# Five small moves in a recurrent attention kernel: halves of a cast, an order of matmuls, filler units, load order, a last projection

## The chip, the cores and the metric

The kernel runs on one core of a Trainium2 chip. The metric is the device time of one execution in microseconds; it is compared by the median of several runs on the same chip. In what follows PE is the matmul engine (TensorE), PEld its weight loads, ACT is ScalarE, DVE is VectorE, POOL is GpSimd, and SP is the engine that issues most of the DMAs.

## The reference

Two branches over the same x of 2048 tokens by 512 are mixed by a gate per token. Branch A is attention with a memory of 8 rows, which is carried from one segment of 32 tokens to the next; branch B is a channel MLP.

```python
g = _sigmoid((x * gate_w).sum(-1, keepdims=True))
# A: 64 segments, one after the other
h = jnp.concatenate([mem, xs], axis=1)            # 8 + 32 rows of 512
q, k, v = (jnp.einsum('btd,dhe->bhte', h, W) for W in (Wq, Wk, Wv))   # 32 heads of 128
scores = jnp.where(mask, jnp.einsum('bhqe,bhke->bhqk', q, k) * scale, -1e9)
o = jnp.einsum('bhqk,bhke->bhqe', _softmax(scores, axis=-1), v)
o = jnp.einsum('bhte,hed->btd', o, Wo)
mem = o[:, :M, :]                                 # feeds the next segment
outs.append(o[:, M:, :])
# B
b = gelu(layernorm(x) @ w1 + b1) @ w2 + b2        # 512 -> 1376 -> 512
return g * a + (1 - g) * b
```

## The kernel before, in words

All weights are loaded once and stay on the chip in bf16. There are two stages, and in both the order of the instructions is written out by hand; each engine runs its own in that order and waits on semaphores for what others make.

**The MLP stage** comes first. It goes over eight blocks of two tiles of 128 tokens, and in each block over eleven chunks (`fc`) of the 1376 hidden columns. `a_mm` makes a chunk (PE, then gelu on ACT into `hTm`, which has two buffers, one for every other block), and `b_mm` multiplies it with w2 two chunks later. For nine of the sixteen tiles (`DEF`) the second product is put off: `spill` writes `hTm` in two pieces to DRAM (`h_dr`), on SP. While the stage runs, SP also issues the loads of the second stage's weights: `loads(blk)` two pieces of 1 MB in each block, at chunk 8, Wv first, then Wq, Wk, and in block 6 the four of Wo. `loads_x(blk)` issues the next two tiles of x into `xt`, which has six buffers, so that a new tile waits until the old one in its buffer was read last, by `gate_sums` (chunk 9, DVE). `prep` makes the layer norm's statistics of the next block on DVE, `prep_tr` transposes its rows on PE.

**The segment loop** has 64 steps `s = 4 T + si`: four segments in each tile T of 128 tokens. Of a segment's 40 rows, 32 (24 tokens and 8 memory rows) are projected within the step, and the other 8 tokens (the "left" ones) of all four segments together, one tile ahead. A step runs as follows:

- Q and K are projected in four units (`QK4`: Q and K of heads 0 to 15, then of heads 16 to 31). After each unit ACT casts 128 x 512 values out of PSUM into `Tb` (`qk_cast`, L134), and DVE transposes them in blocks of 32 into `QT` or `KT` (`qk_tr`, L138). The last of the four is K's second half (`n == 3`).
- `scores(s, 0)` are the scores of heads 0 to 15 (into the bank `SbF`), and ACT makes their exp, E. V is projected in two units. Between them stand three small things: `xsums(E, 0)` (L715), sums of E for the token columns, which only `recip_x` reads much later in the step; `msum(0)` (L816) and `mnorm(0)`, sums and normalisation for the memory columns; and `scores(s, 1)` (L267, into `U[0]`), the scores of heads 16 to 31, which read the second half of `KT`.
- `av` multiplies E with V (and with `VP`, the left tokens' V, which SP moves by `vp_load`), `wo_pass` projects the memory rows by Wo, and `new_mem` transposes the result into `hT`, the input of the next step. `recip_x` sends the token sums through DRAM (`r_dr`, `Rb`), and in the next step `x_norm` on POOL normalises the tokens into `UT` and `UL`.

While PE waits in a step it is given filler: `side(T, si)` is a list of units of work for later, of which `run(n)` takes n at certain places of the step. In steps with si = 2 it is `wo_left` (the projection of the left tokens, eight units); for T = 0 there are none yet, and `mlp_units(8)` stands in. One such unit is one chunk (T, fc) of the second MLP product that was put off: the 32 KB tile `hm`, loaded by SP from `h_dr`, times w2, in two halves of four matmuls of 256 columns. Beside that, the loop takes two or three such halves in every step. `hm` has five buffers; `recip_x` issues as many new loads as chunks were completed since its last call (`hm_load(owed[0])`), and `hm_load4` loads four at once at the start of steps 2 and 60. For the last tile, steps 60 and 61 have `mlp_units(4)`. Over the whole loop all 99 chunks are worked off in the order of the list.

**The last step** has no next one. After its V units the token sums are made with `sums`, UL's unused part is cleared on POOL (L896), and `fill = wo_left(T, X2)` is begun with `run(3)`; then DVE makes the reciprocals (L901), `wo_pass` projects `UT` of the step before, DVE multiplies E by the reciprocals (L905, L906), and `av` follows. The remaining five units of `wo_left` stand behind `av`.

Of the kernel before, what the change touches and what calls it, by code (L numbers as in the profile page):

```python
# [9 lines left out]
FP32 = mybir.dt.float32  # L10
# [18 lines left out]
def kernel(ctx, tc, A_x, A_mem0, A_Wq, A_Wk, A_Wv, A_Wo, A_seg_len, B_x, B_w1, B_b1, B_w2, B_b2, gate_w, out):  # L29
# [272 lines left out]
    with tc.tile_pool(name="mlpw", bufs=1) as mlpw, \  # L302
# [51 lines left out]
        def loads_x(blk):  # L354
            if 2 * blk + 7 < NT:
                ld_x(2 * blk + 6)
                ld_x(2 * blk + 7)

        def loads(blk):
            if blk == 3:  # L360
                nc.sync.dma_start(m0[:], A_mem0[0])

            for kc in range(2 * blk, min(2 * blk + 2, 3 * KC)):
                ld_w(*((Wv_sb, A_Wv), (Wq_sb, A_Wq), (Wk_sb, A_Wk))[kc // KC], kc % KC)
            if blk == 6:
                for i in range(0, H, 8):
                    ld_o(i)
# [187 lines left out]
        for n, (blk, fc) in enumerate(units):  # L555
            a_mm(blk, fc)
            if n == len(units) - 1:
                dummy = msmall.tile([P, 1], FP32, tag="dummy", name="dummy")
                nc.scalar.activation(out=dummy[:], in_=omg[:, 0:1], func=ACTF.Exp)
            if n >= LAG:  # L560
                b_mm(*units[n - LAG])
            if fc == 0:
                if blk >= 1:
                    gates(blk - 1)
                if blk + 1 < NBLK:
                    prep(blk + 1)
                else:
                    gate_sums(blk)
                    for _ in consts():
                        pass  # L570
            if blk + 1 < NBLK:
                f0 = 8
                if fc == 7:
                    spill(blk, 0, 6)
                if fc == 2 and blk >= 1:
                    spill(blk - 1, 6, FC)
                if fc == 3 and blk >= 1:
                    loads_x(blk - 1)
                if fc in (f0, f0 + 1):
                    prep_tr(blk + 1, fc - f0)  # L580
                if fc == f0 + 1:
                    gate_sums(blk)
                if fc == 8:
                    loads(blk)
                if blk == NBLK - 2 and fc == 4:
                    first_h()
            elif fc >= 1:
                if fc == 2:
                    spill(blk - 1, 6, FC)
                if fc == 3:  # L590
                    gates(blk)
                if fc == 7:
                    spill(blk, 0, 6)
# [42 lines left out]
    def side(T, si):  # L636
        gens = []
        if si == 2:
            gens = [wo_left(T - 1, X1) if T >= 1 else mlp_units(8)]
        elif T + 1 == NT:  # L640
            gens = [mlp_units(4)] if si < 2 else []
        else:
            gens = [[left_qk(T + 1, 0, 0, X1), left_qk(T + 1, 1, 0, U[3])], [left_qk(T + 1, 0, 1, X1), left_qk(T + 1, 1, 1, U[3])], [],
                    [left_v(T + 1, 0, X1), left_v(T + 1, 1, U[3])]][si]
        return chain(*gens)
# [122 lines left out]
    for s in range(nseg):  # L768
        T, si = divmod(s, SPT)
        last = s == nseg - 1  # L770
        hc, hn = hT[s % 3], hT[(s + 1) % 3]
        W1, W2, W3 = WS[si]
        fill = side(T, si)
        if s + 1 < nseg:
            prep_h(s + 1)
        if s >= 1:
            x_norm(s - 1)
        if si == 0 and T >= 2:
            c_load(T - 2)
        if si < 3:  # L780
            vp_load(T, si + 1)
        if last:
            c_load(T - 1)
            c_load(T)
        if si == 0 and T + 2 < NT:
            load_xT(T + 2)
        if s in (2, (NT - 1) * SPT):
            hm_load4()
        for n, (t, hf) in enumerate(QK4):
            bk = U[(0, 2, 1, 3)[n]]  # L790
            for kc in range(n == 1, KC):
                qk_unit(bk, hc, t, hf, kc)
                if n == kc == 0:
                    qk_unit(U[2], hc, *QK4[1], 0)
            if n == 0:
                flush(act_q, 9)
                flush(dve_q, 9)
            qk_tr(qk_cast(bk[:]), (QT, KT)[t], hf, LEFT * (1 - t))
            if n == 0:
                mask_put(1)  # L800
        V = cx.tile([P, NG, Dh], BF16, tag="V", name="V")
        E = cx.tile([P, NG, EW], BF16, tag="E", name="E")
        R = cx.tile([P, NG * 40], FP32, tag="R", name="R")
        Rs[s] = R
        xsum = SbF[:, 0:32 * NG].rearrange("p (i q) -> p i q", q=32)

        def exps(i2, x):
            c = slice(0, 40) if x else slice(40, EW)
            nc.scalar.activation(out=E[:, 4 * i2:4 * i2 + 4, c], in_=Sb[i2][:, :, c], func=ACTF.Exp, scale=scale)  # L809

        def msum(i2):
            if i2:
                sums(U[3][:, 320:352].rearrange("p (i q) -> p i q", q=8), E[:, 4:8, :], 40, 48, 8, True)
                return
            for j in range(4):
                nc.tensor.matmul(U[1][32 * j:32 * j + 32, 320:384], lhsT=BO[:, 32 * j:32 * j + 32], rhs=E[:, 0:4, 40:56],  # L816
                                 start=True, stop=True, skip_group_check=True, tile_position=(0, 32 * j))

        def mnorm(i2):
            r, e = RP[i2], E[:, 4 * i2:4 * i2 + 4, 40:56].rearrange("p i (a q) -> p i a q", q=8)  # L820
            if i2 == 0:
                m = U[1][:, 320:384].rearrange("p (i a q) -> p i q a", i=4, a=2)
                nc.vector.tensor_reduce(out=r.rearrange("p (i q) -> p i q", q=8), in_=m, axis=AX.X, op=ALU.add)
            nc.vector.reciprocal(out=r, in_=U[3][:, 320:352] if i2 else r)
            nc.vector.tensor_tensor(out=e, in0=e, in1=r.rearrange("p (i q) -> p i q", q=8).unsqueeze(2).to_broadcast([P, 4, 2, 8]), op=ALU.mult)

        scores(s, 0)
        nc.scalar.activation(out=E[:, 0:4, :], in_=Sb[0], func=ACTF.Exp, scale=scale)
        for kc in range(KC):
            v_unit(X1, hc, 0, kc)  # L830

        def v_cast(vb, h):
            i0 = 4 * vb + 2 * h
            nc.scalar.copy(out=V[:, i0:i0 + 2, :].rearrange("p i e -> p (i e)"), in_=(X1, X2)[vb][:, 256 * h:256 * h + 256])  # L834

        v_cast(0, 0)
        v_unit(X2, hc, 1, 0)
        if not last:
            xsums(E, 0)
            msum(0)  # L840
            mnorm(0)
        scores(s, 1)
        exps(1, 0)
        v_cast(0, 1)
        exps(1, 1)
        for kc in range(1, KC - 1):
            v_unit(X2, hc, 1, kc)
        if not last:
            if s:
                next(mlp, None)  # L850
            msum(1)
            mnorm(1)
        v_unit(X2, hc, 1, KC - 1)
        for h in range(2):
            v_cast(1, h)
        if last:
            break
        run(W1)
        if s:
            next(mlp, None)  # L860
        xsums(E, 1)
        recip_x(s)
        av(s, V, E)
        for j in (0, 2, 1, 3):
            nc.scalar.copy(out=UT[s % 2][:, j, :, 0:M], in_=U[j][:, 0:NG * 40].rearrange("p (i q) -> p i q", q=40)[:, :, 32:40])  # L865
        x_raw(s)
        run(W2)
        prep_q(s + 1)
        w = wo_pass(UT[s % 2], (0, P, 2 * P, Dm), X2)
        if s >= 1:  # L870
            ws[s - 1] = w
        run(W3)
        if si:
            next(mlp, None)
        for _ in extra(T, si):
            pass
        new_mem(w, hn, 0, si)
        run(1)
        new_mem(w, hn, 1, si)
        run(1)  # L880
        new_mem(w, hn, 2, si)
        mlp_outs()
        for _ in fill:
            pass
        if si == 3 and T + 2 < NT:
            left_x(T + 2)
        flush(dve_q, 9)
        nc.vector.tensor_tensor(out=rmin[:, 0:RW], in0=rmin[:, 0:RW], in1=R[:, 0:RW], op=ALU.min)
        flush(act_q, 9)
# [7 lines left out]
    for _ in out_sel(T - 1, X1):  # L897
        pass
    fill = wo_left(T, X2)
    run(3)  # L900
    nc.vector.reciprocal(out=R[:, nx], in_=SbF[:, 0:32 * NG])  # L901
    nc.scalar.activation(out=rmin[:, nx], in_=R[:, nx], func=ACTF.Copy, accum_out=tot[:, 3:4])
    ws[s - 1] = wo_pass(UT[s % 2])
    Rr = R[:, nx].rearrange("p (i q) -> p i q", q=32)
    nc.vector.tensor_tensor(out=E[:, :, 8:40], in0=E[:, :, 8:40], in1=Rr, op=ALU.mult)  # L905
    nc.vector.tensor_tensor(out=E[:, :, 0:8], in0=E[:, :, 0:8], in1=Rr[:, :, 0:8], op=ALU.mult)  # L906
# [176 lines left out]
```

## Time and profile before

| | |
|---|---|
| median of 3 runs | 747.87 us (745.25 to 749.37) |
| the profiled execution | 750.09 us, span 748.2 us |
| mean granted TensorE clock | 0.997 |
| PE, share of the span | 98% |
| ACT, DVE, POOL | 72%, 60%, 33% |
| MLP stage, segment loop | about 73 us, about 672 us |

The span goes from the first to the last instruction of the profiled execution; the time of an execution is some 2 us more. The page gives busy time; matmuls are pipelined, and the end of each is modelled, so that PE counts as busy through a gap that is shorter than the tail of the matmul before it. For such gaps the starts of instructions have to be compared. In the rows of a timeline the first number is the start in us from the span's start, the second the length, then engine, line, operation, the tile written and the tiles read, the shape and how many instructions are merged; in brackets stands the time that the engine was idle before, and what ended that. In a list of waits the numbers are the total in us, how often, and the longest. SPq is SP's instruction queue: a DMA stands there at its issue, not at its landing.

### The profile page before, as it was taken

Reading aid. Unit: us, or ns where it says so; the run is one execution under the profiler, and the core shown is the slowest. Engines: PE = TensorE matmul, PEld = TensorE weight load, DVE = VectorE, ACT = ScalarE, POOL = GpSimd, SP = SyncE. Lnnn points to the kernel's source line nnn. Section 1 sums busy time; section 2 is a strip of 40 time slices with the busy share of each in tenths; the row PEclk is TensorE's granted clock in tenths of the full one; section 3 lists DMA queues with packets and bytes.
Section 4 is the critical chain, followed back from the end, with each engine's and each line's share of the span. In section 5 each row is a group of like instructions: output and inputs, shape, how many; then the busy total and the mean of one; then the engine's idle time right before and its main releaser. Section 6 shows DMA issues by size and latency. Waiting matters only on the chain. (4 is left out here: it accounts for less than half of the span.)

```text
span 748.2 us, 44010 instructions
## 1 busy us (share of the span) xinstructions
PE 732.8 (98%) x19147; PEld 428.8 (57%) x19147; DVE 448.9 (60%) x1541; ACT 536.7 (72%) x1629; POOL 246.6 (33%) x515
## 2 busy tenths in 40 slices
PE   8999998999999999999999999999999999999997
PEld 5776554556565555555555555555555555555553
DVE  6877554656565555656565665556665656555554
ACT  6777765777777777777777777777777777777664
POOL 4001332332334333343234334243333343333331
PEclk9999999999999999999999999999999999999999
DMA  8999222222222323122321323231322313222221
GB/s 308 343 360 360 84 83 55 69 87 80 78 68 62 97 74 93 47 83 80 93 79 38 96 75 97 69 81 57 92 78 82 85 44 94 69 90 70 85 63 61
DMA packets 61944, 76.82 MB, mean 103 GB/s; under 512 B 26729, under 2 KB 51922, under 8 KB 60210
## 3 DMA queue, kind: packets, MB, share of 16 engines
q1 hardware_dynamic: 60802, 72.51, 31.1%
q8 instruction: 151, 2.47, 1.3%
q0 software_dynamic: 400, 0.92, 0.3%
q10 hardware_dynamic: 544, 0.52, 0.2%
q14 instruction: 47, 0.39, 0.2%
HBM read 60.21 MB, written 7.70 MB: 91 GB/s over the span
## 5 line engine op out<-in xcount | busy, mean ns | idle before, releaser
L134 ACT CAST Tb<-U 128x512 bf16<-128x512 f32 x288 | 168.8, 586 | 82.5 <-PE U L129 76.8
L745 POOL TENSOR_TENSOR UT<-XR,Rb 128x384 bf16<-128x384 bf16 x126 | 114.1, 927 | 324.6 <-DMA Rb<-r_dr 228.0
L129 PEld LDWEIGHTS <-hT 128*32 128x32 bf16 x4096 | 108.8, 97 | 97.8 <-issue 2.0
L129 PE MATMUL U<-Wq_sb,hT 128*32 128x512 bf16 x2048 | 145.9, 382 | 0.4 <-DVE hT L763 0.4
L129 PE MATMUL U<-Wk_sb,hT 128*32 128x512 bf16 x2048 | 145.2, 381 | 0.0
L148 PE MATMUL X<-Wv_sb,hT 128*32 128x512 bf16 x2048 | 142.9, 378 | 0.0
L160 PE MATMUL X<-Wo_sb,UT 128*32 128x512 bf16 x2016 | 120.8, 380 | 0.0
L834 ACT CAST V<-X 128x256 bf16<-128x256 f32 x256 | 88.7, 372 | 16.0 <-PE X L148 1.1
L138 DVE STREAM_TRANSPOSE QT<-Tb 128x256 f32<-128x256 f32 x128 | 57.0, 445 | 71.1 <-ACT Tb L134 70.9
L763 DVE CAST hT<-U 128x8 bf16<-128x8 f32 x126 | 20.8, 167 | 130.9 <-PE U L761 96.6
L160 PEld LDWEIGHTS <-UT 128*32 128x32 bf16 x2048 | 56.4, 96 | 55.7 <-issue 16.6
L721 ACT CAST XR<-U 128x256 bf16<-128x256 f32 x252 | 78.6, 438 | 0.0
L752 ACT CAST w<-X 128x128 bf16<-128x128 f32 x189 | 44.8, 310 | 41.7 <-PE X L160 41.0
L138 DVE STREAM_TRANSPOSE KT<-Tb 128x256 f32<-128x256 f32 x128 | 57.0, 445 | 25.9 <-ACT Tb L134 25.9
L737 POOL TENSOR_TENSOR racc<-racc,R 128x128 f32<-128x128 f32 x63 | 28.8, 457 | 105.7 <-DVE R L735 101.1
L148 PEld LDWEIGHTS <-hT 128*32 128x32 bf16 x2048 | 45.2, 95 | 20.6
L689 PE MATMUL W<-w_sb,hm 128*32 128x256 bf16 x728 | 50.5, 273 | 3.6 <-DMA hm<-h_dr 3.6
L865 ACT CAST UT<-U 128x64 bf16<-128x64 f32 x252 | 35.4, 227 | 25.9 <-PE U L296 25.9
L745 POOL TENSOR_TENSOR UL<-XR,Rb 128x128 bf16<-128x128 bf16 x126 | 51.5, 430 | 0.0
L809 ACT ACTIVATE E<-U 128x64 bf16<-128x64 f32 (+1 forms) x128 | 35.0, 273 | 9.3 <-PE U L271 0.4
L484 PEld LDWEIGHTS <-w_sb 128*128 128x128 bf16 (+1 forms) x352 | 34.1, 100 | 10.4
L160 PE MATMUL X<-Wo_sb,UL 128*32 128x512 bf16 x512 | 38.7, 379 | 1.0 <-POOL UL L896 1.0
(184 smaller groups left out, 1250.5 us busy)
## 6 DMA issues: line engine op xcount, KB each, us to landing
Rb<-r_dr SPq DMA_DIRECT2D x63, 512.0 KB, 3.9
Wv_sb<-in_A_Wv_dram SPq DMA_DIRECT2D x4, 1024.0 KB, 7.5
Wq_sb<-in_A_Wq_dram SPq DMA_DIRECT2D x4, 1024.0 KB, 8.5
Wk_sb<-in_A_Wk_dram SPq DMA_DIRECT2D x4, 1024.0 KB, 8.4
Wo_sb<-in_A_Wo_dram SPq DMA_DIRECT2D x4, 1024.0 KB, 12.6
VP<-VL SPq DMA_DIRECT2D x64, 64.0 KB, 3.7
hm<-h_dr SPq DMA_DIRECT2D x91, 32.0 KB, 2.6
c<-c_dr SPq DMA_DIRECT2D x16, 128.0 KB, 4.6
```

Of the source, the lines that this page charges most:

```text
L129: nc.tensor.matmul(bk[32 * j:32 * j + 32, :], lhsT=G[:, kc, :], rhs=W5[t][:, kc, h0:h1, j, :], start=(kc == 0), stop=(kc == KC - 1), tile_ ...
L134: nc.scalar.copy(out=Tb[:], in_=bk.rearrange("p (a b e) -> p a e b", a=8, b=2))
L138: nc.vector.transpose(out=dst[:, 8 * hf:8 * hf + 8, c0:c0 + 32, :].rearrange("p a r b -> p a (r b)").bitcast(FP32), in_=Tb[:].rearrange("p ...
L148: nc.tensor.matmul(bk[32 * j:32 * j + 32, :], lhsT=G[:, kc, :], rhs=Wv5[:, kc, 4 * vb:4 * vb + 4, j, :], start=(kc == 0), stop=(kc == KC - ...
L160: nc.tensor.matmul(bk[32 * c:32 * c + 32, :], lhsT=U_[:, j, i, :], rhs=Wo_sb[:, 4 * i + j, :], start=(n == 0), stop=(n == NW - 1), tile_po ...
L689: nc.tensor.matmul(W[32 * c:32 * c + 32, cc], lhsT=hm[:, 32 * c:32 * c + 32], rhs=w2_sb[:, fc, cc], start=(fc == 0 and h == 0), stop=(fc = ...
L721: nc.scalar.copy(out=XR[:, j], in_=U[j][:, 0:NG * 40].rearrange("p (i q) -> p i q", q=40)[:, :, 0:32])
L745: nc.gpsimd.tensor_tensor(out=out[:, :, 4 * h:4 * h + 4, o:o + b - a], in0=XR[:, :, 4 * h:4 * h + 4, a:b], in1=Rb[:, h, :, :, r:r + b - a] ...
L752: nc.scalar.copy(out=w[:, a:b], in_=bk[:, a:b])
L809: nc.scalar.activation(out=E[:, 4 * i2:4 * i2 + 4, c], in_=Sb[i2][:, :, c], func=ACTF.Exp, scale=scale)
L834: nc.scalar.copy(out=V[:, i0:i0 + 2, :].rearrange("p i e -> p (i e)"), in_=(X1, X2)[vb][:, 256 * h:256 * h + 256])
L865: nc.scalar.copy(out=UT[s % 2][:, j, :, 0:M], in_=U[j][:, 0:NG * 40].rearrange("p (i q) -> p i q", q=40)[:, :, 32:40])
```

## The change

There are five edits.

1. K's last unit (`n == 3`) is cast in two instructions of 256 columns, and transposed in two, each of which needs one cast alone.
2. `xsums(E, 0)` moves behind `scores(s, 1)` on PE.
3. Step 2 has six filler units of the put-off MLP, not eight. The order of the chunks stays, so that all later ones move by two chunks.
4. In the MLP stage the next x tiles are issued at chunk 10 of the block itself instead of chunk 3 of the block after, and the weights of blocks 1 and on behind them at chunk 10, no longer at chunk 8. SP thus issues x, then weights, then the block's second spill; before it was weights, second spill, x.
5. In the last step the first three units of `wo_left` come behind `wo_pass`.

```diff
-                if fc == 3 and blk >= 1:
-                    loads_x(blk - 1)
                 if fc in (f0, f0 + 1):
                     prep_tr(blk + 1, fc - f0)
                 if fc == f0 + 1:
                     gate_sums(blk)
-                if fc == 8:
+                if fc == 8 and blk == 0:
                     loads(blk)
+                if fc == 10:
+                    loads_x(blk)
+                    if blk:
+                        loads(blk)
...
         if si == 2:
-            gens = [wo_left(T - 1, X1) if T >= 1 else mlp_units(8)]
+            gens = [wo_left(T - 1, X1) if T >= 1 else mlp_units(6)]
...
-            qk_tr(qk_cast(bk[:]), (QT, KT)[t], hf, LEFT * (1 - t))
+            if n < 3:
+                qk_tr(qk_cast(bk[:]), (QT, KT)[t], hf, LEFT * (1 - t))
+            else:
+                Tb = ew.tile([P, 8, 32, 2], BF16, tag="Tb", bufs=3, name="Tb")
+                for a in (0, 4):
+                    nc.scalar.copy(out=Tb[:, a:a + 4], in_=bk[:, 64 * a:64 * a + 256].rearrange("p (a b e) -> p a e b", a=4, b=2))
+                for a in (0, 4):
+                    nc.vector.transpose(out=KT[:, 8 + a:12 + a].rearrange("p a r b -> p a (r b)").bitcast(FP32),
+                                        in_=Tb[:, a:a + 4].rearrange("p a e b -> p (a e b)").bitcast(FP32))
...
         if not last:
-            xsums(E, 0)
             msum(0)
             mnorm(0)
         scores(s, 1)
+        if not last:
+            xsums(E, 0)
         exps(1, 0)
...
     fill = wo_left(T, X2)
-    run(3)
     nc.vector.reciprocal(out=R[:, nx], in_=SbF[:, 0:32 * NG])
     nc.scalar.activation(out=rmin[:, nx], in_=R[:, nx], func=ACTF.Copy, accum_out=tot[:, 3:4])
     ws[s - 1] = wo_pass(UT[s % 2])
+    run(3)
```

## The prediction

> **What bounds the kernel now.** I read the page's shares first, then the list of PE's waits, then the timelines of the places that the diff touches.
>
> ```profile
> PE 732.8 (98%) x19147; PEld 428.8 (57%) x19147; DVE 448.9 (60%) x1541; ACT 536.7 (72%) x1629; POOL 246.6 (33%) x515
> DMA  8999222222222323122321323231322313222221
> ```
>
> PE is busy nearly everywhere: time is won only where PE stands still. DMA is full in slices 2 to 4 (about 19 to 75 us) and idle in the main after that, so a delay of transfers counts in that part alone. PE's waits:
>
> ```profile
> PE W L689 <- DMA hm<-h_dr: 3.6, 3, 2.4
> PE X L160 <- POOL UL L896: 1.0, 1, 1.0
> ```
>
> Both belong to places of the change. The step lengths come from the first Wq matmul of a step, in PE's timeline: steps 2, 3 and 4 lie between the first two rows, steps 41, 42 and 43 between the last two.
>
> ```profile
> 93.62 0.40 PE L129 MATMUL U<-Wq_sb,hT 128*32 128x512 bf16 x4
> 130.69 0.39 PE L129 MATMUL U<-Wq_sb,hT 128*32 128x512 bf16 x4
> 503.69 0.40 PE L129 MATMUL U<-Wq_sb,hT 128*32 128x512 bf16 x4
> 534.23 0.40 PE L129 MATMUL U<-Wq_sb,hT 128*32 128x512 bf16 x4
> ```
>
> Three early steps take 37.07 us, three late ones 30.54 us: 6.5 us too much. Here is where (PE and SP timelines, and a table of windows whose last columns are the granted clock, the DMA share and GB/s):
>
> ```profile
> 100.74 0.22 PE L291 MATMUL U<-E,V 32*128 32x40 bf16 x6 [0.45 <-issue]
> 101.90 2.58 SPq L661 DMA_DIRECT2D hm<-h_dr  x3
> 114.32 2.75 SPq L661 DMA_DIRECT2D hm<-h_dr  x4
> 117.96 0.29 PE L689 MATMUL W<-w_sb,hm 128*32 128x256 bf16 x4 [2.41 <-DMA hm<-h_dr]
> 118.60:122.50 3.90, 3.90 (x56) 1.63 (x52) 1.28 (x5) 1.66 (x3) 1.28 (x2) 0.56 0.54 171
> ```
>
> PE waits for hm at the end of step 2 (1.2 us of the 3.6), then 2.41 us in step 3, and right behind that runs at a granted clock of 0.56 for 3.9 us, which loses 0.44 x 3.9 = 1.7 us.
>
> **Six units in step 2.** Counting chunks through the code: when step 2 ends, eight units have used up T=1's eleven chunks, the last two of them loaded only by the x3 issue at 101.90 of that same step; step 3 then needs a chunk out of the x4 issue at 114.32, 3.6 us before. With six units step 2 ends with chunk 8 done; chunks 9 and 10 were loaded in step 2 and are used in steps 3 and 4, and step 3 issues two loads, not four. From there on each chunk is loaded at least a step before its use (but for the four-chunk load of step 60, which stands as it is), so all three waits go, and the slow clock behind them. The two units' matmuls move to steps 61 and 62, at equal cost. What comes late next: the units had also covered ACT's casts of w before `new_mem`.
>
> ```profile
> 729.23 0.71 ACT L752 CAST w<-X 128x128 bf16<-128x128 f32 x3 [0.79 <-PE X L160]
> c_dr<-ct SPq DMA_DIRECT2D x9, 128.0 KB, 3.8
> ```
>
> Three casts take 0.71 us, and two units and a half of filler that stay cover about half: I keep 0.4 us as a new wait, and the 0.45 us "issue" wait at 100.74. Gain: 6.5 - 0.4 - 0.45 = **5.7 us** (if the slow clock came from something else: 4.0). T=15's last chunk now ends in step 62, so its `c_dr` write (3.8 us to landing) and the load of c behind it, which waits on SP, start around 730; a load of the same size takes about as long again (estimate), so c is there near 738, and only the last instructions, after 740, read it. Free. Nothing else is queued on SP behind that wait.
>
> **Halves, and scores ahead of sums.** One step of the steady stretch, all engines:
>
> ```profile
> 517.52 0.58 ACT L134 CAST Tb<-U 128x512 bf16<-128x512 f32 x1 [0.23 <-PE U L129]
> 518.00 0.36 ACT L828 ACTIVATE E<-SbF 128x224 bf16<-128x224 f32 x1
> 518.14 0.45 DVE L138 STREAM_TRANSPOSE KT<-Tb 128x256 f32<-128x256 f32 x1 [0.37 <-ACT Tb L134]
> 518.51 0.19 PE L715 MATMUL SbF<-E,BO 128*32 128x40 bf16 x4
> 518.53 0.20 PE L816 MATMUL U<-E,BO 128*32 128x64 bf16 x4
> 518.64 0.28 PE L267 MATMUL U<-QT,KT 128*32 128x40 bf16 x16
> ```
>
> Matmuls overlap, so starts are to be compared. The token sums (L715, 40 columns) hold PE 0.02 us; the memory sums (L816, 64 columns) should by that hold it 0.03, and the second scores could start at 518.56. They start at 518.64, just behind the end of the last KT transpose (518.14 + 0.45 = 518.59). No busy share shows this 0.08 us, because the earlier matmuls' ends overlap it. Prices for halves, from the nearest rows:
>
> ```profile
> 509.66 0.65 ACT L834 CAST V<-X 128x256 bf16<-128x256 f32 x2
> 514.75 0.61 DVE L144 STREAM_TRANSPOSE KL<-Tb 128x128 f32<-128x128 f32 x2
> L144 DVE STREAM_TRANSPOSE KL<-Tb 128x128 f32<-128x128 f32 x64 | 19.8, 387 | 0.9 <-ACT Tb L134 0.6
> ```
>
> Two casts of 256 columns take 0.65 us against 0.58 for one of 512, so the second half is cast at 518.17 and the exp that follows ends at 518.43 instead of 518.36; the sums need it at 518.51. Covered, with some 0.04 us to spare. A transpose of half the size takes 0.39 with KL's scattered output; into KT's plain rows I estimate 0.31 (0.45 less half of what 256 columns cost beyond a fixed part). The second half is then ready between 518.21 + 0.31 = 518.52 and 518.60. The first eight score matmuls need only the first half (518.3), and the rest come 0.05 us later, near 518.59. So the wait goes in the good case and shrinks in the bad one, where moving the sums behind the scores still hides 0.02. Gain 0.03 to 0.08 a step, I take 0.065 (nearer the plain copy): 63 x 0.065 = **4.1 us**, since in the steady steps PE waits for nothing else that the list shows. Whole range 0 (if both halves cost more than their rows) to 5.0.
>
> **The last projection.**
>
> ```profile
> 734.87 1.80 POOL L745 TENSOR_TENSOR UT<-XR,Rb 128x384 bf16<-128x384 bf16 x2 [6.66 <-DMA Rb<-r_dr]
> 737.38 0.31 POOL L896 MEMSET UL<- 128x256 bf16 x1
> 737.74 0.83 PE L160 MATMUL X<-Wo_sb,UL 128*32 128x512 bf16 x12 [0.96 <-POOL UL L896]
> 738.66 0.22 DVE L906 TENSOR_TENSOR E<-E,R 128x64 bf16<-128x64 bf16 x1
> ```
>
> PE waits 0.96 us for the memset of UL. `wo_pass` reads UT, ready at 736.67, so put first it hides the memset. `av` needs E, ready at 738.88, and comes on PE at about 739.1 after both: E is just early enough. Gain **1.0 us** (at most 1.1; 0.7 if E is what is late next).
>
> **x ahead of the weights.** This part costs. The issue order of SP, and whom it feeds:
>
> ```profile
> 19.87 0.33 SPq L501 DMA_DIRECT2D h_dr<-hTm  x1
> 20.25 0.90 SPq L322 DMA_DIRECT2D Wv_sb<-in_A_Wv_dram  x2
> 24.03 1.03 SPq L318 DMA_DIRECT2D xt<-in_A_x_dram  x2
> 24.32 0.08 DVE L467 DVE_READ_ACCUMULATOR junk<-xt,gw_bc 128x1 f32 x1
> 55.99 0.69 DVE L436 BATCH_NORM_STATS2 st<-xt 128x6 f32<-128x512 bf16 x1 [0.54 <-DMA xt<-in_A_x_dram]
> 71.99 0.65 SPq L189 DMA_DIRECT2D VP<-VL  x1
> 74.00:76.00 2.00, 2.00 (x44) 1.01 (x40) 1.90 (x6) 1.38 (x3) 1.86 (x5) 1.00 1.00 346
> 76.00:78.00 2.00, 2.00 (x84) 1.29 (x80) 0.95 (x3) 1.59 (x4) 0.00 (x0) 1.00 0.45 136
> 79.34 0.19 PE L296 MATMUL U<-E,VP 32*128 32x64 bf16 x4
> h_dr<-hTm SPq DMA_DIRECT2D x9, 192.0 KB, 3.6
> r_dr<-R SPq DMA_DIRECT2D x63, 4.0 KB, 1.8
> ```
>
> The gain is one wait: the statistics of the last block wait 0.54 us for x, which PE feels; with x ahead of 2 MB this goes: -0.5. But an xt buffer is free only when `gate_sums` has read it (24.32 + 0.08), and x cannot go out much sooner than it does today. SP is in order, so in blocks 1 to 4 the weights, and the second spill behind them, now stand behind that wait: they go out at 24.95 instead of 20.25. The spill issued at 19.87 lands at 23.5 (3.6), and the weights followed it without a gap; now they flow from 24.95 + 1.8 (what even a tiny DMA takes). That is 3.25 us later, less 0.7 us for 256 KB of x no longer behind them: **about 2.5 us** of transfer time lost (bounds 0.5 and 4.7). It isn't won back, since the queue is full until about 77. Wo, the spills and VP for step 0 come out of that queue last. VP is at hand at about 78.6 (the share falls at 76 to 78, issue order behind it; estimate) and is read at 79.34. With the change it lands near 81.1, PE is there at 78.7: a new wait of 2.4 us, 1.8 us net. A wait of that length was followed by the slow clock in step 3, so I add the same 1.7 us with it: **+3.5 us**. Wo's own slack at its first use a microsecond later is as large. Gelu may also wait for a late spill of hTm, but that takes from the same 2.5 us.
>
> The Trainium skill, "TensorE: Matmul & The Clock Gate", Part 1, has the clock halved only after an idle window of about 3.4 us; by that rule a wait of 2.4 us costs no clock here, and the result is rival 4. The row of step 3 speaks against it: 2.41 us were enough. The skill's "DMA: Bandwidth & Descriptors", Anatomy of one DMA, fits 436 GB/s (for GpSimd's queue); at that rate the queue would catch up within three blocks, and the result is rival 1. The windows show 346 at a full share, which speaks against it.
>
> **The sum.** -5.7 - 4.1 - 1.0 + 3.5 = -7.3 us. The profiled execution took 750.09 us (748.2 of span), 2.2 above the median of the runs, 747.87. I put the change on the median: **740.6 us**. About 0.5% (3.7 us) is what a measurement can tell here, the three runs lying 4.1 us apart.
>
> **Rivals.** (1) The queue loses little, for it works with gaps that x fills, and VP comes in time: +3.5 becomes -0.5, **736.6 us**. For: the engines' rate dips at times under 346. Against: the share stays near 1.0. Chance 0.24. (2) The halves bring nothing, as the second half of KT is ready no sooner: -3.2, **744.7 us**. For: KL's 0.39 gives 518.60. Chance 0.14. (3) Slower: the halves do not overlap. If ACT's halves run 0.37 each plus a handoff of 0.05 (518.31) and DVE's second half 0.39 from there, KT is ready at 518.74, 0.15 later than now, and the sums that stood before the scores no longer fill 0.02: 0.18 x 63 = 11.3 us lost instead of 4.1 won, -5.7 - 1.0 + 3.5 + 11.3 = +8.1, **756.0 us**. It decides from a loss of 0.05 us a step. Against it stands the row of two casts in 0.65. Chance 0.06. (4) The wait for VP comes without the slow clock: 1.7 less than the forecast, **738.9 us**. For: the 1.2 us of waits in step 2 left the clock alone, and 2.4 lies nearer to the 2.41 that did not only if my 2.5 us hold. Chance 0.18. My forecast has 0.36; 0.02 is left for what I have not seen.
>
> **From this the numbers.** Forecast, rivals 1 and 4 and a fifth of rival 2 are faster by over 0.5%: 0.81. The rest of rival 2 and what is left are within: 0.13. Slower: 0.06. The range runs from a little under rival 1 to a little over rival 2, which leaves out rival 3 and the ends of the bounds: 735 to 746.
>
> **What would show it.** No wait for hm in steps 2 and 3 and no slow clock at 118; scores at L267 starting some 0.03 us after the memory sums and steady steps of three in about 30.35 us; no wait for the memset at the end. A wait for VP near 79 and weights of block 1 issued near 25 would bear out the last part; steps longer than 30.54, or VP in time, would make the forecast wrong on its one or its other side.

## The result and the profile after

The changed kernel takes **812.03 us** (median of 5 runs, 811.86 to 813.6) where the kernel before takes 746.72 on the same chip (5 runs, 745.25 to 749.37): ratio **1.0876, 95% interval 1.0851 to 1.0901**. It is 8.8% slower; 740.6 was forecast, and the range ended at 746.

The page of the changed kernel, shares of the engines and of DMA, against 98% and 748.2 us before:

```profile
span 810.1 us, 44146 instructions
PE 734.6 (91%) x19139; PEld 428.8 (53%) x19147; DVE 461.4 (57%) x1605; ACT 540.7 (67%) x1693; POOL 246.3 (30%) x515
DMA  9899221121222212131213222231223212121222
```

PE is as long busy as before (734.6 us, was 732.8). So no work was added to it: it stands still some 60 us more. Its list of waits says for whom (total, times, longest):

```profile
PE SbF L717 <- DVE E L835: 57.5, 63, 1.3
PE W L691 <- DVE ct L675: 7.6, 8, 1.3
PE U L528 <- POOL ident masks.py:199: 1.5, 1, 1.5
```

Two waits that the kernel before did not have. The first comes in each of the 63 steps, the second in every eighth. The waits for hm (3.6 us) and for the memset (1.0) are gone. Step starts in PE's timeline, the same matmul as in the prediction:

```profile
95.21 0.40 PE L129 MATMUL U<-Wq_sb,hT 128*32 128x512 bf16 x4
540.45 0.40 PE L129 MATMUL U<-Wq_sb,hT 128*32 128x512 bf16 x4
573.99 0.40 PE L129 MATMUL U<-Wq_sb,hT 128*32 128x512 bf16 x4
586.48 0.40 PE L129 MATMUL U<-Wq_sb,hT 128*32 128x512 bf16 x4
```

Three late steps (540.45 to 573.99) take 33.54 us, 11.18 each; they took 30.54, 10.18 each. The step after them takes 12.49. One such step, all engines:

```profile
567.49 0.20 PE L826 MATMUL U<-E,BO 128*32 128x64 bf16 x4
567.52 0.27 PE L267 MATMUL U<-QT,KT 128*32 128x40 bf16 x16
567.62 0.20 PE L271 MATMUL U<-QT,KL 128*32 128x64 bf16 x4
567.80 0.23 DVE L833 TENSOR_REDUCE SbF<-U 128x32 f32<-128x64 f32 x1 [0.31 <-PE U L826]
568.07 0.37 DVE L834 RECIPROCAL SbF<-SbF 128x32 f32<-128x32 f32 x1
568.47 0.22 DVE L835 TENSOR_TENSOR E<-E,SbF 128x64 bf16<-128x64 bf16 x1
568.74 0.22 PE L717 MATMUL SbF<-E,BO 128*32 128x40 bf16 x4 [0.92 <-DVE E L835]
568.77 0.63 PE L148 MATMUL X<-Wv_sb,hT 128*32 128x512 bf16 x8
```

The scores (L267) start 0.03 us behind the memory sums (L826), as the prediction said. But the token sums (L717) behind them stand until `mnorm(0)` has ended on VectorE: reduce, reciprocal and multiply, 0.9 us one after the other, which start only when the memory sums are there. The V units (L148) stand behind the sums in PE's queue. The list names E, which the multiply writes. That is the last thing that VectorE did, but not the thing that was waited for, as the experiments below show: the matmul's output is in **SbF**, and all three of VectorE's instructions have SbF among their operands too.

The other wait, at the start of a tile (s = 44 here; VectorE and PE):

```profile
581.29 0.23 DVE L835 TENSOR_TENSOR E<-E,RS 128x64 bf16<-128x64 bf16 x1
581.43 0.75 DVE L675 TENSOR_SCALAR ct<-W,omg 128x512 bf16<-128x512 f32 x1
582.23 0.29 PE L691 MATMUL W<-w_sb,hm 128*32 128x256 bf16 x4 [0.85 <-DVE ct L675]
```

Moved by two units, the put-off MLP of a tile now ends, every eight steps, with the half that is taken in the middle of the step, and the next half, a few matmuls later, begins a new tile in the same accumulator W. It must wait until VectorE has emptied W (`ct`), and that stands behind `mnorm(1)`.

The account, span against span (+61.9): 63 steps longer by 1.02 are +64; the ct waits are +8.7 (seven of 1.0, one of 1.7); the waits for hm and the slow clock are -6.5; the last step is 0.4 longer; and steps 5 to 62 hold some 4 us less of small irregular delays, which may lie hidden under the new wait (not shown). Sum: +62.6.

### The profile page after: what moved, and what is told of

Same layout as the page of the kernel before. It is cut to its first block, busy times and chain, and to the rows that moved or that the text cites. A ratio compares the mean times of both kernels' runs of the same rounds, so it can differ in the third digit from the quotient of the medians.

```text
span 810.1 us, 44146 instructions
## 1 busy us (share of the span) xinstructions
PE 734.6 (91%) x19139; PEld 428.8 (53%) x19147; DVE 461.4 (57%) x1605; ACT 540.7 (67%) x1693; POOL 246.3 (30%) x515
## 5 line engine op out<-in xcount | busy, mean ns | idle before, releaser
L134 ACT CAST Tb<-U 128x512 bf16<-128x512 f32 x224 | 131.5, 587 | 61.9 <-PE U L129 55.6
L148 PE MATMUL X<-Wv_sb,hT 128*32 128x512 bf16 x2048 | 144.3, 378 | 0.0
L717 PE MATMUL SbF<-E,BO 128*32 128x40 bf16 x504 | 27.4, 192 | 57.5 <-DVE E L835 57.5
L691 PE MATMUL W<-w_sb,hm 128*32 128x256 bf16 x728 | 53.2, 273 | 7.6 <-DVE ct L675 7.6
L717 PEld LDWEIGHTS <-BO 128*32 128x32 bf16 x504 | 22.8, 107 | 67.9 <-issue 63.5
L148 PEld LDWEIGHTS <-hT 128*32 128x32 bf16 x2048 | 47.2, 96 | 20.7
L834 DVE RECIPROCAL RS<-U 128x32 f32<-128x32 f32 x63 | 22.5, 357 | 59.3 <-PE U L281 59.3
L805 ACT CAST Tb<-U 128x256 bf16<-128x256 f32 x128 | 41.4, 375 | 16.3 <-PE U L129 16.3
```

The lines of the kernel that those rows point to most:

```text
L134: nc.scalar.copy(out=Tb[:], in_=bk.rearrange("p (a b e) -> p a e b", a=8, b=2))
L148: nc.tensor.matmul(bk[32 * j:32 * j + 32, :], lhsT=G[:, kc, :], rhs=Wv5[:, kc, 4 * vb:4 * vb + 4, j, :], start=(kc == 0), stop=(kc == KC - ...
L691: nc.tensor.matmul(W[32 * c:32 * c + 32, cc], lhsT=hm[:, 32 * c:32 * c + 32], rhs=w2_sb[:, fc, cc], start=(fc == 0 and h == 0), stop=(fc = ...
L717: nc.tensor.matmul(xs[32 * c:32 * c + 32, h, 0:40], lhsT=BO[:, 0:P:4], rhs=E[:, 4 * h + c, 0:40], start=False, stop=True, skip_group_check ...
L805: nc.scalar.copy(out=Tb[:, a:a + 4], in_=bk[:, 64 * a:64 * a + 256].rearrange("p (a b e) -> p a e b", a=4, b=2))
```

## The experiments

### Where does the sums' wait come from

**e1: the order of scores and sums alone.** All else as in the kernel before.

```diff
-            xsums(E, 0)
             msum(0)
             mnorm(0)
         scores(s, 1)
+        if not last:
+            xsums(E, 0)
```

> The kernel before with one edit only: the token sums stand behind the second scores, and so behind the memory columns' normalisation, as in the changed kernel. Theory (the sums now wait for DVE's write of E's memory columns, which they do not read): every step is 1.01 us longer, as in the changed kernel (11.17 against 10.16), 63 x 1.015 = 64 us: about 811 us. Rival (the halves of the cast and transpose cost the time): about 747 us, no wait of PE for E in the list of waits.

Measured: 805.59 us (one run) against 749.59, undisturbed steps (the shortest, which hold no further wait; the first of each tile is always some 0.3 longer) of 11.17 to 11.21. PE's list:

```profile
PE SbF L715 <- DVE E L825: 50.8, 63, 0.9
```

So this one edit makes nearly the whole loss. **e3: the changed kernel with only this edit undone.**

> The changed kernel with the token sums back ahead of the memory sums, the other four edits kept. Theory: the wait goes, steps of 10.09 to 10.13 us, 744 to 747 us. Rival (halves cost time): steps longer than 10.16 us, over 750 us.

Measured: 754.47 us (752.66 to 757.88), ratio 1.0067 (1.0047 to 1.0087), undisturbed steps of 10.10 to 10.13 us. The edit costs some 60 us in this surrounding too. The total is 7 us over the upper end of what I expected: the four other edits together still lose 5 us, because the ct waits (8.8 us, 8 times) take more than the rest wins.

**e2: `mnorm(0)` written behind the sums**, with PE's order as in the changed kernel.

```diff
             msum(0)
-            mnorm(0)
         scores(s, 1)
         if not last:
             xsums(E, 0)
+            mnorm(0)
```

> The changed kernel, PE's order untouched; only the normalisation of E's memory columns (DVE) is written behind the token sums in the program. Theory: the sums no longer wait, steady steps of about 10.09 us (0.07 under the kernel before, since scores follow the memory sums at once), 812 - 63 x 1.08 = about 744 us. Rival (the sums wait for something real, such as the bank that exp reads): stays near 812 us. Second rival (the normalisation, now behind the sums, makes av late): 750 us or more, with waits at L291 for E.

Measured: 764.17 us (763.63 to 765.97), ratio 1.0198 (1.0166 to 1.023). The sums wait no more, but steps take 10.29 us, not under 10.1, and the total is 20 us over my theory. The timeline shows the same wait turned round:

```profile
502.99 0.19 PE L717 MATMUL SbF<-E,BO 128*32 128x40 bf16 x4
503.37 0.23 DVE L833 TENSOR_REDUCE SbF<-U 128x32 f32<-128x64 f32 x1 [0.54 <-PE SbF L717]
```

Now VectorE's reduce waits for the sums, though it reads nothing that they write: it reads U and writes SbF. E is then late for the products (2.8 us in all by the list, and a gap of about 0.2 a step). Program order decides who waits; that somebody does is a property of the pair.

My theory up to here was that the sums' rows of E lie within the stretch that the strided multiply writes. **e8: the multiply by rows**, so that no stretch of E is shared.

```diff
-            nc.vector.tensor_tensor(out=e, in0=e, in1=r...
+            if i2 == 0:
...
+                for i in range(4):
+                    nc.vector.tensor_tensor(out=e[:, i], in0=e[:, i], in1=rb[:, i]..., op=ALU.mult)
...
```

> The kernel after with one edit: the multiply of mnorm(0), which writes columns 40 to 55 of four rows of E at once, is written as four multiplies, one a row; program order and PE's order as in the kernel after. Theory (the sums wait because their rows lie inside the stretch from the first to the last element of the one strided write, though not a column is shared): no wait L717 <- E any more, steady steps of 10.1 to 10.3 us (VectorE has about 0.4 us more to do a step, E may come late to the attention products by a part of it), eight ct waits as before: 752 to 764 us. Rival A (the tile E as a whole is tracked, or the sums need something else that VectorE does late): the wait stays or grows, steps of 11.2 to 11.6 us, 812 to 840 us.

Measured: 824.01 us (one run), steps of 11.36 to 11.40; the wait stays, and grows with the longer chain:

```profile
PE SbF L717 <- DVE E L838: 69.9, 63, 1.1
```

That theory is refuted. What e1, e2 and e8 have in common is SbF: `mnorm(0)` keeps its 32 sums and reciprocals in columns 336 to 367 of this PSUM bank (`RP`, L255), and the token sums go into other columns of it. **e9: the scratch in SBUF.**

```diff
-    RP = [SbF[:, 336:368], RS[:]]
+    RS0 = ep.tile([P, 32], FP32)
+    RP = [RS0[:], RS[:]]
```

> The kernel after with one edit: the 32 columns of scratch in which mnorm(0) keeps its sums and reciprocals lie in SBUF instead of in columns 336 to 367 of SbF, the PSUM bank into which the token sums write. E, the program order and PE's order stay. Theory (what the sums wait for is the bank SbF, which VectorE's chain uses as scratch, not E: the run with the multiply by rows kept the wait though its rows share nothing with the sums): the wait L717 <- E goes, mnorm(0) waits for no sums either, steady steps of 10.07 to 10.12 us, eight ct waits and the late VP as in the run with the sums put back: 750 to 754 us. Rival (E as a whole tile is what is tracked): nothing changes, steps of 11.17, 812 us.

Measured: 759.55 us (758.52 to 764.03), ratio 1.0143 (1.0107 to 1.018). The wait is gone, and the shortest steps take 10.06 us. Groups by line, PE and VectorE (total, mean ns, idle before):

```profile
L718 PE MATMUL SbF<-E,BO 128*32 128x40 bf16 x504 | 26.6, 183 | 0.2 <-issue 0.2
L836 DVE TENSOR_TENSOR E<-E,RS 128x64 bf16<-128x64 bf16 x126 | 42.1, 334 | 13.5 <-ACT V L845 0.5
```

It is 5 us more than I expected, and the second row points to a reason: the multiply has become slower. The row holds the multiplies of both `mnorm(0)` and `mnorm(1)`; taken one by one from the timeline, the 63 of `mnorm(0)`, whose scratch was moved, take 366 ns in the mean, where each took 220 with the scratch in SbF. **e13: the scratch in another PSUM bank**, U[1], into which PE writes next only for the products, which need this multiply anyway.

```diff
-    RP = [SbF[:, 336:368], RS[:]]
+    RP = [U[1][:, 384:416], RS[:]]
...
-        for i2 in (1, 0):
-            nc.vector.tensor_copy(out=R[:, 32 * i2:32 * i2 + 32], in_=RP[i2])
+        nc.vector.tensor_copy(out=R[:, 32:64], in_=RP[1])
...
+            if i2 == 0:
+                nc.vector.tensor_copy(out=R[:, 0:32], in_=r)
```

> The kernel after with mnorm(0)'s scratch in columns 384 to 415 of U[1], another PSUM bank, which PE next writes in the attention products (they wait for this multiply anyway); its copy into R stands right behind the multiply. Theory (same bank is what serialises; a scratch in PSUM keeps the multiply at 0.22 us beside GpSimd): no wait of the sums for VectorE, multiply 0.22 us each time, steady steps of 10.07 to 10.12 us, eight ct waits and the late VP stay: 751 to 755 us, some 6 us under the run with the scratch in SBUF. Rival (any scratch in PSUM makes the sums wait): steps of 11.2, 812 us. Rival 2 (the copy makes the products late): steps of 10.2 to 10.3, 758 to 765 us.

Measured: 756.97 us (756.53 to 759.78), ratio 1.0102 (1.0068 to 1.0137). That is 2 us over the upper end of my theory. No wait of the sums either, and the multiply of `mnorm(0)` (second row) is back at its time:

```profile
L834 DVE TENSOR_TENSOR E<-E,RS 128x64 bf16<-128x64 bf16 x63 | 18.6, 296 | 6.6
L834 DVE TENSOR_TENSOR E<-E,U 128x64 bf16<-128x64 bf16 x63 | 13.9, 221 | 6.5
```

But steps now take 10.17 to 10.20: the copy beside the multiply makes `mnorm(1)` late for the products' second half (by 0.12 us in step 35, against the same step of e9), which is a part of rival 2. **Shown:** what makes PE and VectorE wait for each other is that both use SbF, whatever the columns; neither E nor PSUM as such does. SbF names a tile and the bank that it lies in; which of the two counts the runs do not tell. The Trainium skill, "PSUM — Partial Sum Buffer", PSUM bank collisions raise a hardware error, says that a matmul's write and a VectorE access to the same bank and the same 32 partitions must not meet, disjoint columns or not, and that the hardware does not arbitrate. The runs show what that becomes here, an order kept by semaphores, at 0.9 us a step; no run shows what the chip would do without that order.

### The side units

**e4: e2 with eight side units instead of six.**

```diff
-            gens = [wo_left(T - 1, X1) if T >= 1 else mlp_units(6)]
+            gens = [wo_left(T - 1, X1) if T >= 1 else mlp_units(8)]
```

> As the changed kernel with the normalisation behind the sums, but eight units in step 2 again. Theory (the shift by two chunks moves the end of each tile's MLP to the middle of a step, where PE waits 1.0 us for DVE to empty W, eight times): these eight waits go, the waits for hm in steps 2 and 3 and the slow clock come back (up to 5.7 us): about 2 us under the run with six units. Rival (the wait for W comes of the late sums alone): 4 to 6 us over the run with six units.

Measured: 755.94 us (754.17 to 759.31), ratio 1.0085 (1.0053 to 1.0118). That is 8.2 us under e2 by the medians (4.8 by the spans of the two profiles): six units cost more than the 2 us I expected. The ct waits are gone (10.3 us in e2's list), the waits for hm are back (3.2), and so is the slow clock (0.51 and 0.64 at 120 to 124 us).

**e7: seven units**, with halves and the moved projection, all else as in the kernel before. By the count of chunks a tile then ends before the products, and its successor starts behind the output projection.

> The kernel before with halves, the last projection moved, and seven side units in place of eight (six in the change). Counted through the code, a tile's MLP then ends in the middle of a step, before the attention products, and its successor starts only behind the output projection, so VectorE's read of W has the time between and PE should not wait for ct. Theory: the waits for hm in step 3 and the slow clock behind them go (2.4 + 1.7 us; the 1.2 us at the end of step 2 may stay), no wait L691 <- ct: 4 to 5 us under the kernel with halves and the projection alone, about 741 against 749.6 for the kernel before. Rival (the wait for ct comes with any number under eight): eight waits of 1.0 to 1.3 us, 3 to 5 us over the kernel with halves and the projection alone.

Measured: **746.37 us (743.92 to 748.08) against 750.61, ratio 0.9945 (0.992 to 0.9969)**. No wait for ct is in its list, the waits for hm are 0.2 us in all, and the clock stays full. VectorE is done with W (first row, 113.04) 0.64 us before PE writes into it again, and 0.7 to 1.0 us before in the seven later tiles:

```profile
112.29 0.75 DVE L673 TENSOR_SCALAR ct<-W,omg 128x512 bf16<-128x512 f32 x1
113.68 0.30 PE L689 MATMUL W<-w_sb,hm 128*32 128x256 bf16 x4
```

So it was not "fewer than eight" that hurt, but where in the step the tile ends. The total missed my theory of 741: by the medians e7 is 1.3 us under e5 below, the same with eight units, and not 4 to 5, and the intervals overlap. In the profiles steps 2 to 4 take 31.1 us against 34.4 in e5.

### x ahead of the weights

**e6: this edit alone.**

> The kernel before with x ahead of the weights only. Theory: block 1's weights go out at about 24.4 us instead of 20.3, VP for step 0 about 2 us later, PE waits for it at step 0 some 1.5 to 2.4 us, no slow clock behind it, and the wait of 0.54 us of the statistics for x goes: 1.0 to 1.9 us slower, 750.6 to 751.5 against 749.6. Rival A (prediction: the slow clock follows): 3.5 us slower, 753.1. Rival B (the queue loses nothing): 0.5 us faster, 749.1.

Measured: 751.88 us (749.47 to 756.33), ratio 1.0016 (0.9991 to 1.0042): 1.2 us, not to be told from none. SP's and PE's timeline, and behind them the window that follows (the granted clock is the third column from the end):

```profile
24.72 0.90 SPq L322 DMA_DIRECT2D Wv_sb<-in_A_Wv_dram  x2
81.10 0.21 PE L296 MATMUL U<-E,VP 32*128 32x64 bf16 x4 [1.65 <-DMA VP<-VL]
```

```profile
82.00:86.00 4.00, 3.85 (x44) 1.56 (x40) 0.00 (x0) 1.66 (x8) 0.00 (x0) 0.58 0.33 88
```

In the profiled execution all of the prediction's term is there: weights at 24.72, a wait of 1.65 us for VP, and a granted clock of 0.58 for 4 us behind it; step 0 takes 13.70 us instead of 10.39, 3.3 more (3.5 was forecast). Against it, hm is less late in step 3 (1.3 us), and the slow clock there is absent: steps 2 to 4 take 34.1 us instead of 37.1, so that the delay in step 0 is nearly made good. In the changed kernel itself the wait for VP is hidden behind the sums' wait; it shows in e2 (1.5 us), e4 (1.4) and e13 (2.1), all without a slow clock behind it.

### Halves, the last projection, and what can be won

**e5: halves and the moved projection alone. e12: the moved projection alone. e15: the moved projection and seven units, no halves.**

> The kernel before with two edits only: K's last cast and transpose in halves, and the last projection moved. Theory (steps of 10.10 to 10.13 us with the sums back at their place came from the halves): steady steps of about 10.12 us, 63 x 0.05 = 3.2 us less, the three waits for hm as in the kernel before, no wait for the memset, 0 to 1 us from the last projection: 745.5 +- 1 against 749.6 for the kernel before. Rival A (the shorter steps came from the sums' or the side units' rearrangement, halves bring nothing): 749.0, steps of 10.17. Rival B (the prediction's full 0.065 a step and 1.0): 744.5.

> The kernel before with the last projection moved only. Seen so far: in the six kernels that have it (all with the halves too) the last step's computation ends 13.4 to 13.5 us after the step's start instead of 14.7, but the program's end follows 4.5 to 4.9 us behind VectorE's last instruction instead of 3.0. Theory A (the longer tail is of the moved projection, through the order or place of the last instructions): tail of 4.5 us or more here, the span gains nothing: 749.6 to 751 where the kernel before has 750.6. Theory B (it comes with the halves): tail of 3.0, 1.3 us faster. In both the wait for the memset of UL is gone.

> The kernel before with seven side units and the last projection moved, no halves. Theory A (the longer end comes with the halves and takes back most of what they win, 0.03 us x 63 = 1.9 us less 1.5): end of 3.0 to 3.1 us behind VectorE's last instruction, ratio 0.993 to 0.996, level with the run that has the halves. Theory B (the halves win 3 us): ratio 0.998 to 1.000.

Measured: e5 747.68 us (745.53 to 750.04), ratio 0.9959 (0.9937 to 0.9981). e12 747.83 (744.83 to 750.59), ratio 0.9985 (0.9963 to 1.0008). e15 745.99 (743.95 to 747.46), ratio 0.9954 (0.9937 to 0.9971), level with e7, which has the halves. The projection wins what it was meant to: in e12 the list has no wait for the memset, and VectorE's last instruction ends 14.1 us behind the last step's start instead of 15.2. The halves shorten the undisturbed step from 10.15 to 10.10; the times of whole kernels do not show it (e7 to e15, 0.7 us, within both intervals). Theory B of e15 is refuted. Theory A's account (a longer end eats the gain) holds for these profiles alone: from VectorE's last instruction to the end of the span it is 3.0 us before and 4.5 in e5, but 3.2 in e14 below, which has the halves too.

**e10: halves, sums behind the scores with the scratch in SBUF, projection, seven units. e11: the same with the sums ahead. e14: as e10, with the scratch in U[1] as in e13.**

> Halves, scores ahead of token sums with the scratch in SBUF, the last projection moved, seven side units, loads as in the kernel before. Theory: as the run with seven units (746.4 against 750.6 for the kernel before on that chip, ratio 0.9945), less 0.00 to 0.03 us a step from the sums behind the scores: ratio 0.990 to 0.995, 743 to 746.5. Rival (the sums behind the scores make E or the exps late for something else): steps of over 10.15, ratio over 0.997.

> The same with the sums left ahead of the scores. Theory: the scratch's place costs or wins nothing by itself where program order already has the sums first (no wait in the list of the run with seven units is for SbF): steps of 10.10, ratio 0.9945 +- 0.002. If the order of scores and sums is worth 0.03 a step as predicted, this kernel is 1.9 us slower than the one with the order changed; if it is worth 0.00, the two agree.

> Halves, scores ahead of token sums with the scratch in U[1], the last projection moved, seven side units, loads as in the kernel before. Theory: as the run with seven units (ratio 0.9945 to the kernel before), less 0.02 to 0.03 us a step: ratio 0.9915 to 0.9945. Rival (the order of scores and sums brings nothing, or the copy costs as much): 0.9945 to 0.998.

Measured: e10 749.59 us (748.05 to 752.97), ratio 1.0022 (1.0001 to 1.0042); e11 751.48 (749.32 to 753.61), 1.0033 (1.001 to 1.0056); e14 745.72 (744.2 to 747.95), **0.9951 (0.9932 to 0.997)**. Against e7, e11 has nothing but the scratch in SBUF, and loses about 0.9% by it: I expected the place to cost nothing, and e10, which has it there too, missed its forecast (0.990 to 0.995). Between e10 and e11 only the order of scores and sums differs: the undisturbed step is 10.07 with the scores ahead and 10.10 without, and the medians are 1.9 us apart, as the 0.03 us a step of my expectation would have it; the intervals of the two ratios overlap. e11's timeline, a step with GpSimd at work, and its groups:

```profile
538.27 1.80 POOL L746 TENSOR_TENSOR UT<-XR,Rb 128x384 bf16<-128x384 bf16 x2 [5.76 <-ACT E L837]
539.35 0.81 DVE L834 TENSOR_TENSOR E<-E,RS 128x64 bf16<-128x64 bf16 x1
540.53 0.40 DVE L834 TENSOR_TENSOR E<-E,RS 128x64 bf16<-128x64 bf16 x1
540.98 0.20 PE L292 MATMUL U<-E,V 32*128 32x40 bf16 x4 [0.21 <-DVE E L834]
```

```profile
L834 DVE TENSOR_TENSOR E<-E,RS 128x64 bf16<-128x64 bf16 x126 | 40.7, 323 | 13.8 <-ACT E L818 0.9
```

The multiply of `mnorm(0)` takes 0.81 us beside GpSimd's product, so that of `mnorm(1)` ends only at 540.93, and PE waits for it. In e14, where the multiply is short but the copy stands behind it, undisturbed steps take 10.17 to 10.20, and the sums behind the scores bring nothing that can be measured, as my rival had it: e14, e7 and e15 agree within their intervals. All three beat both kernels. e15 does it with two edits of one line each, seven units and the moved projection.

## Why the prediction was wrong

**Scores ahead of token sums: the step that failed.** The prediction costed it as an order of PE's matmuls: "moving the sums behind the scores still hides 0.02". But the move passes `mnorm(0)` as well, which stands between them in the text and is on another engine, and which shares a PSUM bank with the sums. I had read the row of `SbF<-E,BO` and asked only what PE did beside it. The rows of VectorE that show SbF as an output and an operand of `mnorm(0)` stand in the trace of before, in the same step as the rows that the prediction shows:

```profile
518.85 0.23 DVE L823 TENSOR_REDUCE SbF<-U 128x32 f32<-128x64 f32 x1 [0.27 <-PE U L816]
519.12 0.37 DVE L824 RECIPROCAL SbF<-SbF 128x32 f32<-128x32 f32 x1
519.52 0.22 DVE L825 TENSOR_TENSOR E<-E,SbF 128x64 bf16<-128x64 bf16 x1
```

There the sums (518.51) come first and nobody waits for SbF; written behind these three, as in the changed kernel, they start when the multiply has ended. Price: 1.0 us x 63, fifteen times the term of 4.1 with which it shared a line. The rival on the slower side (halves that do not overlap, 756.0) had the sign but neither the mechanism nor the size. The prediction weighed two rules of the Trainium skill, on the clock and on the DMA rate; the rule on PSUM banks that is quoted above, which spoke against this change, it did not.

**Six units.** The waits for hm went, as forecast: steps 2 to 4 are free of their 6.5 us (35.22 us from 95.21 to 130.43, which are three steps of 11.18 and the first ct wait of 1.7). Of these 6.5, the 1.7 us of slow clock are in part luck of the profiled execution: e5 and e12 have waits of nearly the same length (2.25 and 2.35 us), and the clock stays full. The step that failed is "The two units' matmuls move to steps 61 and 62, at equal cost". They move the end of every tile by two chunks through all 60 steps between, into a place where PE asks for W 0.7 us after the tile's last half (580.69 to 581.38 in step 44), while VectorE's reading alone takes 0.75 us and stands behind `mnorm(1)`: +8.7 us. In the kernel before, PE came back to W 4 us after VectorE was done. By this account the term is +2.2 instead of -5.7, and by e2 against e4 even +8.2. Seven units keep most of the gain without the price: 3.4 us in the profiles' steps 2 to 4 (e5 to e7), 1.3 us by the medians, with intervals that overlap.

**Halves.** The mechanism was right (no list names a wait for the second half, and rival 3 did not come), and so was the size in an undisturbed step: halves make it 0.05 us shorter (10.15 to 10.10), the scores ahead of the sums another 0.03 (10.10 in e11 to 10.07 in e10, which has no wait for SbF), together the 0.08 at the upper end of the prediction. What failed is to multiply it by 63 for the whole kernel: there the halves bring 0 to 2 us, and rival 2 (they bring nothing) is nearer. In the profile of e5 the longer end of the program takes 1.4 us of it; where the rest goes is open.

**The last projection.** -1.0 forecast; the work ends 1.1 us sooner in e12, and the measured ratio (-1.1 us) agrees without excluding zero. Right.

**x ahead of the weights.** The chain of reasoning held link by link in e6: issue time, late VP, a wait (1.65 where 2.4 was forecast, 1.5 and 2.1 elsewhere), the slow clock. What was wrong is that the slow clock must follow; it came in one of the four traces with such a wait of 1.4 us or more (e6, but not e2, e4 and e13; the last section says what parts them). The kernel as a whole loses 1.2 us (-0.7 to +3.1) instead of 3.5.

The total was wrong by 71 us, and by the runs that lack the edit some 60 of them are the sums' place alone. Without that, with seven units and the old order of loads, the kernels stand at -3.6 to -4.2 us (e15, e14, e7).

## What to carry to other kernels

Before an instruction is moved, list every instruction of every engine between its old place and its new one, and for each the memory that it touches by bank, not by column: here PE and VectorE, on one PSUM bank, waited for each other in program order. When a wait is named after a tile, read the other operands of both rows before believing the name. When filler is shortened, follow where its boundaries fall in all later steps, for a boundary may carry an instruction of another engine.

## What was not expected of the hardware

- PE and VectorE were kept apart where both used the PSUM bank SbF in different columns: 57.5 us of waits with the scratch in SbF, none with it in U[1] or in SBUF.
- A small VectorE multiply is not the same beside GpSimd when both inputs lie in SBUF: `mnorm(0)`'s takes 221 ns with one of them in PSUM (e13, 63 times, 222 at most), and 366 in the mean with both in SBUF (e9 and e11). There it takes 226 ns where GpSimd computes no product at the time, and 402 (e9) or 414 (e11) in the mean where it does, up to 0.98 us. The Trainium skill, "SBUF — State Buffer", Who interferes with whom, has this: a VectorE instruction with two SBUF inputs contends with GpSimd's reads. The traces agree.
- Waits of PE of much the same length were followed by a slow clock or not: 2.41 us in step 3 before, 2.18 in e4, 1.65 in e6 (for VP) and 1.85 in e9 (for ct, at 717 us) were; 2.25 in e5, 2.35 in e12 and 2.13 in e13 (for VP) were not. What parts them in the traces is where the wait lies. In every trace the granted clock changes only at times that are whole multiples of 3.413 us apart (before: at 6.37, 119.01, 122.43 and 747.07 us, the last three 33, 34 and 217 multiples after the first), and between the start and the end of the work each slow stretch is one such window long. Here are the window with the long wait and the one behind it, before and in e12 (PE's busy time is the second number, the granted clock the third from the end):

```profile
115.60:119.01 3.41, 1.05 (x36) 0.67 (x40) 0.46 (x4) 0.99 (x4) 0.00 (x0) 1.00 0.39 97
119.01:122.43 3.42, 3.42 (x40) 1.37 (x32) 0.98 (x4) 1.37 (x3) 1.21 (x2) 0.50 0.48 148
```

```profile
116.61:120.03 3.42, 1.93 (x52) 1.09 (x56) 0.71 (x4) 0.58 (x1) 0.00 (x0) 1.00 0.56 153
120.03:123.44 3.41, 3.41 (x85) 1.82 (x80) 1.96 (x5) 2.60 (x5) 2.27 (x4) 1.00 0.37 102
```

Before, the wait lies inside one window, in which PE is busy for 1.05 us; in e12 a border cuts it. In the windows ahead of the four slow stretches PE was busy for 1.05 (before), 1.23 (e4), 1.57 (e9) and 1.77 us (e6); in those that hold most of the waits without one for 1.79 (e13), 1.93 (e12) and 2.14 (e5). The limit is not sharp by this count: 1.65 us in one window of the changed kernel (305.36 to 308.77), with two shorter waits in it, had no slow stretch behind it. No run was made to test this. The Trainium skill, "TensorE: Matmul & The Clock Gate", Part 1, has a window of about 3.4 us that runs freely; the traces agree.

- The end of the program, behind VectorE's last instruction, takes 3.0 to 3.2 us in seven of the kernels (before, e1, e6, e12 to e15), 3.5 in e8 and 4.5 to 4.9 in the other nine, without any computing instruction in it. In the trace's records the difference lies behind the branch after the last test (VectorE's next record starts 0.6 us after it before, 3.0 in e5). It is not of any one edit here; its cause is open.
